# The last 64 queries of four heads as four 64x64 quarters of TensorE's array

## The chip, the cores and the metric

One of the cores of a Trainium2 chip runs the whole program. The metric is the device time in microseconds (us). The kernel before took 1368.56 us (median of 3 runs, 1368.39 to 1369.04).

## The reference

Attention in which each query keeps its 32 largest scores, and then a gated network without a nonlinearity, all in fp32. The shapes are 8 batches, 8 heads, 576 queries and keys, 64 numbers a head; 4608 tokens, 512 wide, with an inner width of 1024.

```python
scores = scale * np.matmul(q, k.transpose(0, 1, 3, 2))
kth = np.partition(scores, -top_k, axis=-1)[..., -top_k:-top_k + 1]
scores = np.where(scores >= kth, scores, -1000000000.0)
attn = softmax(scores)                  # along the keys
x = (attn @ v), heads side by side      # 4608 x 512
a = x @ w1
b = x @ w2
h = a * b @ w3
return h @ w_out
```

## The kernel before

**Slots.** Attention goes in slots of 128 rows of scores for two heads. Two heads make a pair (rows 0 to 63 of a loaded tile are the 64 numbers of one head, rows 64 to 127 those of the other; `HEADS` in line 25 are these two halves). 576 queries are four blocks of 128 and a rest of 64, so a pair has four ordinary slots (t = 0 to 3), and the rests of two pairs, four heads in all, share one slot, t == 4. It is called the shared slot here. In `SLOTS` (line 27) it stands fifth of nine, so of 144 slots 16 are shared ones, counted from 0 these are slots 4, 13, 22, ... 139.

**Scores.** `scores` (line 182) makes the 128 x 2 x 576 scores of a slot in two halves of 288 keys, each in a PSUM tile `st` of two banks; index `a` names the bank. In an ordinary slot bank 0 takes the head of rows 0 to 63 and bank 1 that of rows 64 to 127; each matmul uses 64 rows and all 128 columns of the array (line 197). In a shared slot `a` names the pair: the loaded `qt` has 128 more columns, 512 to 639, in which the host has put the rest of the first head in the upper 64 rows and left columns, and that of the second head in the lower rows and right columns, with zeros elsewhere. One matmul of all 128 rows and 128 columns (line 194) then gives both heads of a pair: the first head's queries on PSUM partitions 0 to 63, the second's on 64 to 127. A matmul in fp32 stands as two in the trace, so the four of a shared slot are eight there.

**The way of a slot.** ACT copies the scores to SBUF (`s`), one copy a half. DVE finds the 32 largest of each row (`top`, with a work tile `w`), POOL makes the threshold (`edge`), ACT and POOL mask (`pab`), ACT takes the exponentials in place, POOL and DVE invert the sums (`sums`). PE turns the weights (`tp`, `ro`), ACT copies them (`pts`, `pr`), PE multiplies them with v (`values`, tile `ro`, in tiles of 128 rows and 64 columns) and spreads the inverted sums over the partitions; ACT copies these (`rec`), and DVE multiplies both into x (`xt`).

**The order.** All engines work through their instructions in the order in which the loop of line 484 writes them. One turn of the loop takes slot i's scores, finds the top 32 of slot i-1, masks slot i-2 and turns and multiplies slot i-3. Between these, `fill` (line 447) puts in 32 matmuls a turn of the network of a batch whose attention is finished (`ab` for the first two products, `eo` for the last; lines 500, 511, 531), so that nothing of the network is left but that of the last batch, which runs alone at the end. In the first turns, before a batch is finished, weights are unpacked instead (`warm`). Three PSUM tiles, `st` for both halves and `tp`, take turns in two buffers of pool `ps_a`: the second `st` of a turn waits for ACT's copy `pts` of this turn's `tp`.

**The loads.** `load_pair` (line 172) loads q, k and v of a pair with one DMA each on SP's queue, three pairs ahead.

Of the kernel before, what the change touches and what calls it, by code (L numbers as in the profile page):

```python
# [9 lines left out]
F32 = mybir.dt.float32  # L10
# [8 lines left out]
B, H, S, D = 8, 8, 576, 64  # L19
NHP = H // 2  # L20
HS = S // 2
# [3 lines left out]
HEADS = slice(0, 64), slice(64, 128)  # L25
# [31 lines left out]
def attn_moe(ctx: ExitStack, tc: tile.TileContext, q, k, v, w1, w2, w3, w_out, out, flag, general):  # L57
# [12 lines left out]
    pe, act, dve, pool, sp = nc.tensor, nc.scalar, nc.vector, nc.gpsimd, nc.sync  # L70

    const = ctx.enter_context(tc.tile_pool(name="const", bufs=1))
    kq_p = ctx.enter_context(tc.tile_pool(name="kq", bufs=AHEAD))
# [9 lines left out]
    ident = const.tile([128, 128], F32, name="ident")  # L83
# [13 lines left out]
    if not general:  # L97
        pe, act, dve, pool, sp = (InOrder(tc, e) for e in (pe, act, dve, pool, sp))
# [70 lines left out]
    def at(x, b, *i):  # L169
        return x[(b, *i)] if isinstance(b, int) else x[(ds(b, 1), *i)].rearrange("o p n -> (o p) n")  # L170

    def load_pair(b, hp):

        qt = kq_p.tile([128, 5 * 128], F32, tag="q", name="qt")
        sp.dma_start(qt, at(q, b, hp))
        kt = kq_p.tile([128, S + 64], F32, tag="k", name="kt")
        sp.dma_start(kt, at(k, b, hp))
        vt = kq_p.tile([128, 11 * D], F32, tag="v", name="vt")
        sp.dma_start(vt, at(v, b, hp))
        return qt, kt, vt  # L180

    def scores(pairs, t):

        out = []
        for lo, hi in HALVES:
            st = ps_a.tile([128, 2, 512], F32, tag="a", name="st")
            for a in range(2):  # L190
                cut = slice(lo + 64, hi + 64) if a == 0 else slice(lo, hi)
                if t == 4:
                    qt, kt, _ = pairs[a]
                    pe.matmul(st[:, a, :HS], qt[:, 512:640], kt[:, cut], start=True, stop=True)
                else:
                    (qt, kt, _), p = pairs[0], HEADS[a]
                    pe.matmul(st[:, a, :HS], qt[p, t * 128 : (t + 1) * 128], kt[p, cut], start=True, stop=True)
            out.append(st)
        return out

    def new_s():
        return att_p.tile([128, 2, S], F32, tag="s", name="s", bufs=3)
# [49 lines left out]
    def new_weights():  # L252
        return att_p.tile([128, 2, S], F32, tag="pab", name="pab"), small.tile([128, 2], F32, tag="sums", name="sums")
# [31 lines left out]
    def take_turned(tp, ro):  # L285
        pts = att_p.tile([128, 2, 512], F32, tag="pts", name="pts", bufs=1)
        act.copy(pts, tp)
        pr = att_p.tile([128, 128], F32, tag="pr", name="pr")
        act.copy(pr, ro[:, :128])
        return pts, pr  # L290

    def values(vts, t, pts, pr, sums, ro):

        ov, rb = ro[:, 128:256], ro[:, 256:384]
        ends = t == 4
        for a, h in enumerate(HEADS):
            if ends:
                for j in range(2):
                    pe.matmul(
                        rb[h, j * 64 : j * 64 + 64], sums[:, j : j + 1].to_broadcast([128, 64]), ident[:, h], start=True, stop=True  # L300
                    )
            else:
                pe.matmul(rb[h], sums[:, a : a + 1].to_broadcast([128, 64]), ident, start=True, stop=True)
        for j in range(2 if ends else 1):
            vt = vts[j]
            for c in range(5):
                for i, h in enumerate(HEADS):
                    block = i * 4 + c if c < 4 else (((8, 10), (10, 9))[j][i] if ends else 8 + i)
                    n = slice(i * 64, i * 64 + 64) if ends else slice(0, 128)
                    rhs = pr[:, n] if c == 4 else pts[:, j if ends else i, c * 128 + n.start : c * 128 + n.stop]  # L310
                    to = ov[h, j * 64 : j * 64 + 64] if ends else ov[h]
                    pe.matmul(to, vt[:, block * D : (block + 1) * D], rhs, start=(c == 0), stop=(c == 4))
        return ov, rb
# [91 lines left out]
    if general:  # L405
# [3 lines left out]
        with tc.For_i(0, B, 1) as b:  # L409
            seen = small.tile([1, 1], I32, tag="seen", name="seen", bufs=1)  # L410
            nc.sync.dma_start(seen, flag[ds(b + 1, 1), :])
            with tc.If(nc.values_load(seen, min_val=0, max_val=1) > 0):
                kv, xs = {}, {}
                for hps, t in SLOTS:
                    for hp in hps:
                        if hp not in kv:
                            kv[hp], xs[hp] = load_pair(b, hp), new_xt()
                    s, st = new_s(), scores([kv[hp] for hp in hps], t)
                    for h in range(2):
                        take_scores(s, st, h)  # L420
                    edge = top32_exact(s)
                    pab, sums = new_weights()
                    for a in range(2):
                        mask(s, edge, pab, a)
                        exps(edge, pab, sums, a)
                    invert(sums)
                    tp, ro = turn(pab)
                    ov, rb = values([kv[hp][2] for hp in hps], t, *take_turned(tp, ro), sums, ro)
                    store_x([xs[hp] for hp in hps], t, ov, take_rb(rb))
                xt, parts = [xs[hp] for hp in range(NHP)], ([], [])  # L430
                for pair in range(2):
                    split_x(parts, xt, 0, pair)
                for _ in moe_steps(b, xt, parts, lambda f: f()):
                    pass
# [20 lines left out]
    def pairs_of(i):  # L455
        return [kv[u] for u in slots[i][0]]

    def fetch_pair(u):
        if u < B * NHP:
            kv[u] = load_pair(u // NHP, u % NHP)  # L460
# [23 lines left out]
    for p in range(-1, n_slots + 3):  # L484
        i, j, m = p + 1, p - 1, p - 2
# [28 lines left out]
        if i < n_slots:  # L514
            st = scores(pairs_of(i), slots[i][1])
            ss[i] = new_s()
            take_scores(ss[i], st, 0)
# [4 lines left out]
        if 0 <= m < n_slots:  # L522
            us, t = slots[m]
            for u in us:
                if u not in xts:
                    xts[u] = new_xt()
            ov, rb = values([kv[u][2] for u in us], t, pts, pr, pabs[m][1], ro)
            rec = take_rb(rb)
# [79 lines left out]
```

## Time and profile before

| | |
|---|---|
| median of 3 runs | 1368.56 us (1368.39 to 1369.04) |
| the profiled execution | 1368.85 us, of which the span of its instructions 1367.1 us |
| PE busy | 1269.8 us (93%) |
| DVE busy | 1156.8 us (85%) |
| ACT busy | 981.7 us (72%) |
| POOL busy | 784.6 us (57%) |
| mean granted clock of TensorE | 0.961 of full speed |

The profile is of one execution. A busy engine is one with an instruction in work. Time between instructions counts as idle, and the trace names what ended it. Idle time costs only where the engine is the one that all others come to wait for, and this differs between the start, the long middle and the end of this program.

### The profile page before, as it was taken

The numbers are of one execution on the slowest core, as the hardware profiler recorded it, in microseconds if no ns is written. First come the engines' busy times: TensorE is split into PE (matmuls) and PEld (weight loads), VectorE is DVE, ScalarE is ACT, GpSimd is POOL, SyncE is SP. The second block draws the span as 40 slices with busy tenths as digits, with TensorE's granted clock in tenths as the row PEclk, the third lists the DMA queues.
The fourth block names the chain that finished last, engine by engine and source line by source line (L and its number), as shares of the span: only waits on it lengthen the run. The fifth ranks groups of instructions, "written<-read, shape, count | busy, mean of one in ns | idle before, by whom it ended". The sixth has DMA issues, their size and how long they took to land.

```text
span 1367.1 us, 31053 instructions
## 1 busy us (share of the span) xinstructions
PE 1269.8 (93%) x11025; PEld 1101.1 (81%) x11025; DVE 1156.8 (85%) x4060; ACT 981.7 (72%) x2169; POOL 784.6 (57%) x1033
## 2 busy tenths in 40 slices
PE   2788855899999999999999999999999999999996
PEld 1444434798889998999988899989999889999996
DVE  6989898999999999898989899999899898988000
ACT  4777777777777777786777777777778777777221
POOL 3666677665665656565656565665656565646220
PEclk6889977999999999999999999999999999999998
DMA  6443430002010101001010202011111001000000
GB/s 220 109 131 100 124 104 31 31 12 68 12 59 21 49 31 40 29 21 60 17 63 12 68 12 68 12 48 32 44 36 38 31 17 64 12 19 1 18 18 21
DMA packets 34745, 65.01 MB, mean 48 GB/s; under 512 B 3860, under 2 KB 12052, under 8 KB 34580
## 3 DMA queue, kind: packets, MB, share of 16 engines
q1 hardware_dynamic: 34580, 62.93, 14.5%
q8 instruction: 89, 1.46, 0.4%
q14 instruction: 76, 0.62, 0.1%
HBM read 53.48 MB, written 9.44 MB: 46 GB/s over the span
## 4 chain that ended last, share of the span: by engine, by line
PE 79%; DVE 12%; ACT 5%; issue 2%; POOL 1%; DMA 0%; DVEq 0%; SPq 0%; POOLq 0%; ACTq 0%
PE ab L48 30%; PE eo L48 15%; PE ro L48 14%; PE st L48 11%; PE tp L48 8%; DVE w L48 5%; DVE top L48 3%; ACT pab L48 2%; DVE y L48 2%; DVE z L48 1%; ACT pts L48 1%; PE pf L48 1%; ACT y L48 1%; POOL wl L48 0%; ACT t L48 0%
## 5 line engine op out<-in xcount | busy, mean ns | idle before, releaser
L48 POOL TENSOR_TENSOR pab<-s,pab 128x576 f32<-128x576 f32 x288 | 403.2, 1422 | 251.0 <-DVE w L48 192.9
L48 DVE MAX8 top<-w 128x8 f32<-128x192 f32 (+1 forms) x1152 | 466.3, 445 | 0.0
L48 PE MATMUL ab<-xf,wh 128*128 128x288 f32 x2048 | 432.5, 299 | 0.0
L48 PEld LDWEIGHTS ab<-xf,wh 128*128 128x128 f32 x2048 | 332.8, 188 | 8.3 <-issue 7.4
L48 PE MATMUL ab<-xf,wl 128*128 128x288 f32 x1024 | 309.8, 303 | 0.0
L48 ACT ACTIVATE pab<-s,edge 128x576 f32<-128x576 f32 x288 | 208.0, 771 | 116.3 <-POOL edge L48 116.0
L48 DVE MATCH_REPLACE8 w<-top,w 128x192 f32<-128x192 f32 x864 | 288.7, 341 | 0.0
L48 PE MATMUL st<-kt,qt 64*128 64x288 f32 (+1 forms) x1152 | 206.0, 445 | 60.6 <-ACT pts L48 50.9
L48 ACT ACTIVATE pab<-pab,edge 128x576 f32<-128x576 f32 x288 | 224.8, 781 | 20.9 <-POOL pab L48 20.4
L48 PE MATMUL eo<-g,wf 128*128 128x288 f32 x1536 | 228.2, 300 | 0.0
L48 PEld LDWEIGHTS eo<-g,wf 128*128 128x128 f32 x1536 | 208.3, 188 | 7.0 <-issue 7.0
L48 PEld LDWEIGHTS st<-kt,qt 64*128 64x128 f32 (+1 forms) x1152 | 113.6, 193 | 113.7 <-ACT pts L48 59.6
L48 PEld LDWEIGHTS ab<-xf,wl 128*128 128x128 f32 x1024 | 192.2, 188 | 4.8 <-issue 4.8
L48 ACT COPY s<-st 128x576 f32<-128x576 f32 x288 | 181.8, 632 | 14.1 <-PE st L48 14.0
L48 ACT COPY pts<-tp 128x1024 f32<-128x1024 f32 x144 | 145.4, 1010 | 61.9 <-PE tp L48 57.1
L48 PE MATMUL tp<-ident,pab 128*128 128x128 f32 x1152 | 154.1, 277 | 15.6 <-ACT s L48 15.0
L48 POOL TENSOR_TENSOR g<-whole,g 128x288 fp32r<-128x288 f32 x128 | 102.8, 803 | 114.0 <-ACT g L48 110.1
L48 DVE TENSOR_TENSOR w<-w,s 128x384 f32<-128x384 f32 x288 | 159.9, 555 | 4.9
L48 PE MATMUL ro<-pts,vt 128*64 128x128 f32 (+1 forms) x2560 | 163.3, 273 | 0.0
L48 DVE TENSOR_TENSOR w<-s 128x384 f32<-128x384 f32 x288 | 155.9, 581 | 7.9 <-ACT s L48 7.9
L48 PEld LDWEIGHTS tp<-ident,pab 128*128 128x128 f32 x1152 | 135.8, 143 | 24.7 <-POOL wo L48 13.2
L48 PEld LDWEIGHTS ro<-pts,vt 128*64 128x64 f32 x2560 | 143.7, 144 | 0.0
(49 smaller groups left out, 1275.8 us busy)
## 6 DMA issues: line engine op xcount, KB each, us to landing
z<-in_w SPq DMA_DIRECT2D x64, 256.0 KB, 2.7
vt<-in_v SPq DMA_DIRECT2D x32, 352.0 KB, 3.9
qt<-in_q SPq DMA_DIRECT2D x32, 320.0 KB, 2.9
kt<-in_k SPq DMA_DIRECT2D x32, 320.0 KB, 3.5
out_t<-osb SPq DMA_DIRECT2D x64, 144.0 KB, 1.7
z<-in_wo SPq DMA_DIRECT2D x16, 256.0 KB, 5.0
flag<-missed SPq DMA_DIRECT2D x1, 0.0 KB
seen<-flag SPq DMA_DIRECT2D x1, 0.0 KB
```

Of the source, the lines that this page charges most:

```text
L48: ins = fn(*args, **kw)
```

## The change

The zero-filled copy of the rests is gone from the host's array: `qt` has 576 columns now, and the rests are its last 64. A shared slot takes eight matmuls of 64 rows and 64 columns in place of four of 128 and 128. For the first pair (a = 0) head i lies on rows i and columns i of the array's halves, as before. For the second pair head i's scores go to the other half of the columns, and so to the other half of PSUM's partitions (`HEADS[i ^ a]`). The four matmuls of a half thus lie on four different quarters of the array. In `values` the second pair's turned weights and sums are read from the swapped halves; the count and sizes of the matmuls there stay.

```diff
     def load_pair(b, hp):

-        qt = kq_p.tile([128, 5 * 128], F32, tag="q", name="qt")
+        qt = kq_p.tile([128, S], F32, tag="q", name="qt")
         sp.dma_start(qt, at(q, b, hp))
...
                 if t == 4:
                     qt, kt, _ = pairs[a]
-                    pe.matmul(st[:, a, :HS], qt[:, 512:640], kt[:, cut], start=True, stop=True)
+                    for i, p in enumerate(HEADS):
+                        pe.matmul(st[HEADS[i ^ a], a, :HS], qt[p, 512:], kt[p, cut], start=True, stop=True)
...
                     pe.matmul(
-                        rb[h, j * 64 : j * 64 + 64], sums[:, j : j + 1].to_broadcast([128, 64]), ident[:, h], start=True, stop=True
+                        rb[h, j * 64 : j * 64 + 64], sums[:, j : j + 1].to_broadcast([128, 64]), ident[:, HEADS[a ^ j]],
+                        start=True, stop=True,
                     )
...
-                    n = slice(i * 64, i * 64 + 64) if ends else slice(0, 128)
+                    n = HEADS[i ^ j] if ends else slice(0, 128)
...
     qt = _np.asarray(q).reshape(B, NHP, 2, S, D).transpose(0, 1, 2, 4, 3)
-    qp = _np.zeros((B, NHP, 2, D, 640), _np.float32)
-    qp[..., :512] = qt[..., :512]
-    qp[:, :, 0, :, 512:576] = qt[:, :, 0, :, 512:]
-    qp[:, :, 1, :, 576:] = qt[:, :, 1, :, 512:]
...
-        "in_q": c(qp.reshape(B, NHP, 128, 640)), "in_k": c(kp.reshape(B, NHP, 128, S + 64)), "in_v": c(vp.reshape(B, NHP, 128, 11 * D)),
+        "in_q": c(qt.reshape(B, NHP, 128, S)), "in_k": c(kp.reshape(B, NHP, 128, S + 64)), "in_v": c(vp.reshape(B, NHP, 128, 11 * D)),
```

This is the order on PE in the program before, in a shared slot of the second batch: the network's matmul ahead of the scores, both halves of the scores (`st` with two buffer numbers; two `qt` and `kt` are the two pairs), and the spreading of the sums behind them. Sizes are those of the result.

```order
L48 MATMUL ab_2498<-xf_2408,wh1_99 128x288
L48 MATMUL st_2513<-kt_1419,qt_1417 128x288
L48 MATMUL st_2513<-kt_2056,qt_2054 128x288 [waits DMAHW7_49,DMAHW0_49]
L48 MATMUL st_2516<-kt_1419,qt_1417 128x288 [waits Activation_49]
L48 MATMUL st_2516<-kt_2056,qt_2054 128x288
L48 MATMUL ro_2490<-ident_85,sums_2374 64x128 [waits DVE_49,Activation_49]
```

The same place now:

```order
L48 MATMUL ab_2506<-xf_2416,wh1_99 128x288
L48 MATMUL st_2521<-kt_1423,qt_1421 64x288 x2
L48 MATMUL st_2521<-kt_2064,qt_2062 64x288 [waits DMAHW7_49,DMAHW0_49]
L48 MATMUL st_2521<-kt_2064,qt_2062 64x288
L48 MATMUL st_2526<-kt_1423,qt_1421 64x288 [waits Activation_49]
L48 MATMUL st_2526<-kt_1423,qt_1421 64x288
L48 MATMUL st_2526<-kt_2064,qt_2062 64x288 x2
L48 MATMUL ro_2498<-ident_85,sums_2382 64x128 [waits DVE_49,Activation_49]
```

Each matmul has become two, the waits stand on the first of the two, and what comes before and behind is the same. On DVE, ACT and POOL no instruction moves, and on SP only the size of the q loads differs.

## Rows read from the trace of the kernel before

**Rows 1.** Stretches, with each engine's busy time, granted clock, DMA share, GB/s
```profile
core 0: us, PE busy (x) PEld busy (x) DVE busy (x) ACT busy (x) POOL busy (x), PEclk, DMA share, GB/s
0.00:259.00 259.00, 174.71 (x1010) 106.52 (x1011) 227.57 (x719) 181.55 (x429) 164.50 (x228) 0.82 0.36 109
259.00:1256.00 997.00, 997.00 (x9244) 897.67 (x9243) 915.76 (x3303) 770.90 (x1669) 594.23 (x773) 1.00 0.11 35
```
**Rows 2.** PE's waits from 0 to 259: total us, times, longest
```profile
PE st L48 <- ACT pts L48: 50.9, 17, 6.4
```
**Rows 3.** PE's waits from 259 to the end, all of them
```profile
PE ro L48 <- ACT pr L48: 0.2, 1, 0.2
```
**Rows 4.** Chain that ended last, pieces from its start: start, us, what
```profile
1.21 3.57 DMA kt<-in_k
...
43.09 1.93 DVE w L48 x3
...
167.84 0.52 DVE top L48 x2
...
246.73 1.34 DVE top L48 x2
...
251.43 1.33 PE st L48 x4
```
**Rows 5.** PE in order of time, a shared slot: start, us, what
```profile
479.53 0.29 PE L48 MATMUL ab<-xf,wh 128*128 128x288 f32 x1
479.67 2.10 PE L48 MATMUL st<-kt,qt 128*128 128x288 f32 x8
481.70 0.44 PE L48 MATMUL ro<-ident,sums 128*64 128x128 f32 x4
```
**Rows 6.** PE in order of time, the ordinary slot behind it
```profile
488.38 0.29 PE L48 MATMUL ab<-xf,wl 128*128 128x288 f32 x1
488.61 1.24 PE L48 MATMUL st<-kt,qt 64*128 64x288 f32 x8
489.78 0.44 PE L48 MATMUL ro<-ident,sums 128*64 128x128 f32 x4
490.05 1.04 PE L48 MATMUL ro<-pts,vt 128*64 128x128 f32 x16
490.92 0.39 PE L48 MATMUL ro<-pr,vt 128*64 128x128 f32 x4
```
**Rows 7.** Weight loads by shape: count, busy us, mean ns, idle before
```profile
L48 PEld LDWEIGHTS ro<-pts,vt 128*64 128x64 f32 x2560 | 143.7, 144 | 0.0
L48 PEld LDWEIGHTS st<-kt,qt 64*128 64x128 f32 x1024 | 89.8, 193 | 101.8 <-ACT pts L48 53.3 <-issue 29.9 <-ACT s L48 6.6
```
**Rows 8.** PE in order of time, slot 25, the whole and from its second round
```profile
284.19 1.29 PE L48 MATMUL st<-kt,qt 64*128 64x288 f32 x8
...
284.53 0.70 PE L48 MATMUL st<-kt,qt 64*128 64x288 f32 x4
```
**Rows 9.** DVE's waits for ACT's `rec`, 479 to 562: total, times, longest
```profile
DVE xt L48 <- ACT rec L48: 4.9, 4, 1.6
```
**Rows 10.** DVE in the shared slot that begins at 553.17
```profile
557.08 0.29 DVE L48 TENSOR_TENSOR xt<-ro,rec 128x128 f32<-128x128 f32 x1 [1.16 <-ACT rec L48]
```
**Rows 11.** ACT in the shared slot at 479.67 and the slot behind it
```profile
483.27 0.27 ACT L48 COPY rec<-ro 128x128 f32<-128x128 f32 x1 [0.51 <-PE ro L48]
...
487.19 1.02 ACT L48 COPY pts<-tp 128x1024 f32<-128x1024 f32 x1 [0.44 <-PE tp L48]
```
**Rows 12.** ACT's `pts` and PE's scores, three slots behind a shared one
```profile
503.97 1.00 ACT L48 COPY pts<-tp 128x1024 f32<-128x1024 f32 x1
...
504.75 1.24 PE L48 MATMUL st<-kt,qt 64*128 64x288 f32 x8
```
**Rows 13.** DVE's waits from 256 to 290, all of them
```profile
DVE sums L48 <- POOL sums L48: 2.0, 2, 1.1
```
**Rows 14.** ACT's `pts` in slot 25
```profile
283.67 1.00 ACT L48 COPY pts<-tp 128x1024 f32<-128x1024 f32 x1
```

## The prediction

> **What bounds the kernel now.** I read the stretches first. From 0 to 259 us PE is busy for 174.71 us of 259 and DVE for 227.57; from 259 to 1256 PE is busy for 997.00 us of 997.00, at the full granted clock of 1.00, and DVE for 915.76 [rows 1]. The table of waits says the same from the other side: until 259 PE waited 50.9 us for ACT's `pts` alone [rows 2], and from there to the end 0.2 us in all [rows 3]. The chain in order of time gives the border: its pieces are DVE's and ACT's up to 246.73, and PE's from 251.43 on [rows 4]. So what PE is spared behind the border shortens the program unless another engine becomes late; what it is spared ahead of it should not.
>
> A shared slot comes every nine slots. Two of the sixteen lie at the start (slots 4 and 13, at 42 and 168 us), one right behind the border (slot 22, at 259), and thirteen in the stretch that PE fills.
>
> **The scores of a shared slot.** Before, eight instructions of 288 columns follow each other: from the start of the first to the start of what comes next 481.70 - 479.67 = 2.03 us, 0.25 us each [rows 5]. In an ordinary slot eight instructions of 288 columns take 489.78 - 488.61 = 1.17 us [rows 6], too little for eight after each other: two are at work at once, one on each half of the rows, in four rounds. Halves of the columns do so too: the sixteen of `ro<-pts`, with 128 moving columns, take 490.92 - 490.05 = 0.87 us, and alone they would need 16 x 0.25 x 128/288 = 1.78 us [rows 6]. The order on the engine puts two instructions of one tile ahead of the two of the other tile, and they still overlap, so an instruction that must wait for its own tile does not hold up one of another tile.
>
> The change makes sixteen instructions, four on each quarter. Nothing in this trace runs on quarters; what it shows is rows overlapping and columns overlapping, each with different moving data and at full rate. If both hold at once, the four quarters run four rounds, as an ordinary slot does. I take that as the likeliest. The price, with the entry into the tiles included, is measured from the last matmul of the network: 481.70 - 479.53 = 2.17 us for a shared slot [rows 5] and 489.78 - 488.38 = 1.40 us for an ordinary one [rows 6], so 0.77 us less. The first round of an ordinary slot is longer than the later ones, 284.53 - 284.19 = 0.34 us [rows 8], since the second weights are not there yet; weights of 64 columns load in 144 ns and of 128 in 193 [rows 7], so the new slot is 0.05 us better here. Two more tiles to start cost a few hundredths at most, an estimate from the 0.05 us. Gain per shared slot: between 0.77 and 0.82 us; I take 0.80. The bound on the other side, quarters that do not overlap, is a rival below.
>
> One statement goes further than these rows: the Trainium skill ("TensorE: Matmul & The Clock Gate", Part 3) says that row and column tiles compose, with some 4 ns for each further tile; by it the two further tiles cost under 0.01 us and the gain is 0.81 us. No run here shows it yet.
>
> **Does the gain stay?** In the thirteen slots the question is what restarts from PE and what does not. DVE stands idle in a shared slot until ACT's `rec` arrives, 1.16 us in the one at 553.17 [rows 10] and up to 1.6 us in four such waits [rows 9]. ACT's `rec` itself waited 0.51 us for PE's `ro`, and in the next slot ACT's `pts` 0.44 us for PE's `tp` [rows 11]. With PE 0.80 us earlier, `rec` is 0.80 earlier, and DVE's idle time there falls to 1.16 - 0.80 = 0.36 us: it still waits for PE, and so its long chain of the next slots starts earlier by the same amount. That matters, since three slots behind a shared one `pts` ends at 503.97 + 1.00 = 504.97 and the second half of the scores wants its buffer at 504.75 + 0.34 + 0.24 = 505.33 (a first and a later round): only 0.36 us of slack [rows 8, 12]. Both move together, and the slack stays. Over the long run DVE has room: 915.76 of 997 us [rows 1], so 81 us idle, and the change takes away some 11.
>
> Slot 22 is different. From 256 to 290 DVE waits twice, 2.0 us in all, and only for POOL [rows 13]; it is catching up from the start and does not begin earlier when PE does. In slot 25 `pts` ends at 283.67 + 1.00 = 284.67 [rows 14], and the second half of the scores follows at 284.53 + 0.24 = 284.77 [rows 8]. PE can come earlier by 0.1 us there and no more: of slot 22's 0.80 us I count 0.1.
>
> Slots 4 and 13: the chain has DVE at 43.09 and at 167.84 [rows 4], and PE waits for `pts` behind both. I count 0; the bounds are 0 and 0.8 each, if a wait turns out to hang on these scores.
>
> **The loads.** Each q is 288 KB, not 320. All but the first are three pairs ahead, under PE's work. The first scores wait for k, 3.57 us [rows 4], while q and k, 640 KB, come together; a twentieth of that is 0.18 us at most, and 0.1 is my value (0 to 0.18). In `values` counts and sizes stay, only the halves that are read differ: 0.
>
> **The sum.** 13 x 0.80 + 0.1 + 0.1 = 10.6 us. The profiled execution took 1368.85 us, 1.75 more than its span, and becomes 1358.25. The median is 0.29 lower than that execution: 1358.0 us.
>
> **Rivals.**
>
> Two at a time. In each half the first two matmuls, heads of one pair, use different rows and write the same bank of PSUM, on different partitions; in ordinary slots the two row halves always write different banks. If the banks, not the partitions, decide, only two of the quarters that differ in their bank run together: sixteen instructions in eight rounds, the 2.03 us of before. On top come the entry into the tiles, (488.61 - 488.38) - (479.67 - 479.53) = 0.09 us [rows 5, 6], and half of the 0.10 us by which a first round is longer: 13 x 0.14 = 1.8 us, less the 0.1 of the load, so 1370.3 us. The Trainium skill has this as a rule ("TensorEngine Tiling (Array Packing)", Restrictions and Gotchas, Gotcha 1): different row tiles cannot access the same PSUM bank at the same time. By it the sum would be this rival's. Against it speaks that on any one partition the two writers here have different banks, just as in an ordinary slot. No row of this trace has two row halves in one bank, so it keeps a chance of 0.11.
>
> One at a time, the case that ends slower. If an instruction on a quarter has to wait until the one on the neighbouring quarter is through, be it for the same rows or the same columns, sixteen go after each other: 16 x 0.25 = 4.0 us in place of 2.03, with the 0.14 some 2.1 us more per shared slot, and 14 x 2.1 = 29 us: 1397 us. It decides from the first shared slot on, and the scores would then take twice as long as before. Against it: halves that share all columns, and halves that share all rows, both overlap now [rows 6]. Chance 0.05.
>
> The quarters overlap, and the gain is taken back by DVE's chain. If something in the chain from `rec` over DVE, POOL and ACT to `pts` does not move with PE, the buffer of the second half is late from the third slot on, and a shared slot keeps only the slack of 0.36 us: 13 x 0.36 + 0.2 = 4.9 us, 1363.7 us. For it: in some slots DVE has no idle time at all, and 0.36 us is all that stays of its wait at 553. Against it: that wait, as far as the rows go, ends with PE. Chance 0.07.
>
> **How the numbers follow.** My forecast, four at a time and the gain kept, has 0.77. Its own range is 1355.5 (0.82 us kept fourteen times, and up to 1.5 us at the start) to 1360.0 (0.70 us if the start of four tiles costs a tenth more). The range is 1355.5 to 1366.0: it holds this case and the one in which DVE takes the gain back, 0.84 together, less a little that falls outside. Differences of 0.2%, 2.7 us, are about what can be told from no change. Faster by more than that: 0.77 + 0.07 = 0.84. Within: two at a time, 0.11. Slower: one at a time, 0.05.
>
> **What would show it.** Right, if the sixteen `st` instructions of a shared slot in the middle take about 1.1 to 1.2 us from the first to the start of `ro`, if the slot is then some 8.15 us long and not 488.61 - 479.67 = 8.94 [rows 5, 6], and if PE from 259 on still waits for next to nothing. In slot 25 PE should wait some 0.7 us for `pts`, for the first time. DVE's wait for `rec` in the shared slot that now begins at 553 should be 0.3 to 0.4 us. Wrong, if the sixteen take 2 us or 4, which is the first rival or the second; or if PE waits for `pts` in the third slot behind each shared one, which is the third. If the start up to slot 22 is shorter by more than 0.3 us, I was wrong about what its chain hangs on.

## The result and the profile after

The changed kernel takes 1356.16 us (median of 6 runs, 1355.88 to 1356.86), the kernel before 1368.80 in the same comparison (median of 6 runs). The ratio is 0.9909, with a 95% interval of 0.9898 to 0.9919: 12.6 us less, where 10.6 were forecast.

A shared slot of the changed kernel, on PE in order of time (start, us, what), the counterpart of [rows 5]:

```profile
477.35 0.29 PE L48 MATMUL ab<-xf,wh 128*128 128x288 f32 x1
477.58 1.20 PE L48 MATMUL st<-kt,qt 64*64 64x288 f32 x16
478.71 0.44 PE L48 MATMUL ro<-ident,sums 128*64 128x128 f32 x4
...
550.27 1.20 PE L48 MATMUL st<-kt,qt 64*64 64x288 f32 x16
```

Sixteen instructions take 478.71 - 477.58 = 1.13 us to the next work, where eight took 2.03. From the network's last matmul it is 478.71 - 477.35 = 1.36 us against 2.17: 0.81 us less, 0.01 more than forecast. The distance from this shared slot to the next is 550.27 - 477.58 = 72.69 us, where it was 553.17 - 479.67 = 73.50 before ([rows 5], and the row of 553.17 below): the same 0.81 us over nine slots, so nothing of it is given back in between. All thirteen shared slots behind slot 22 gain it, each within 0.01 us.

That four run at once can be seen in the starts. A window of this slot that ends 0.04 us behind the first score (at 477.62) holds four instructions, and the next four begin 0.29 us behind the first:

```profile
477.58 0.47 PE L48 MATMUL st<-kt,qt 64*64 64x288 f32 x4
...
477.87 0.42 PE L48 MATMUL st<-kt,qt 64*64 64x288 f32 x4
```

Some of the following rows are of windows that end inside a slot's scores; only their first numbers, the starts, are used. The kernel before, with the starts of slots 22, 31 and 58 and the end of slot 25's scores:

```profile
259.11 0.41 PE L48 MATMUL st<-kt,qt 128*128 128x288 f32 x1
...
285.41 0.40 PE L48 MATMUL ro<-ident,sums 128*64 128x64 f32 x6
...
332.66 0.65 PE L48 MATMUL st<-kt,qt 128*128 128x288 f32 x2
...
553.17 2.10 PE L48 MATMUL st<-kt,qt 128*128 128x288 f32 x8
```

Slots 22 and 31 in the changed kernel:

```profile
258.75 0.47 PE L48 MATMUL st<-kt,qt 64*64 64x288 f32 x4
...
332.20 0.70 PE L48 MATMUL st<-kt,qt 64*64 64x288 f32 x6
```

From slot 22 to slot 31 it is 73.55 us before and 73.45 after: of the 0.81 us that slot 22 itself gained, 0.10 stays. Where the rest goes is on PE in slots 23 and 25 of the changed kernel:

```profile
266.80 1.54 PE L48 MATMUL st<-kt,qt 64*128 64x288 f32 x8
268.27 0.44 PE L48 MATMUL ro<-ident,sums 128*64 128x128 f32 x4
...
283.24 0.76 PE L48 MATMUL st<-kt,qt 64*128 64x288 f32 x4
284.17 0.76 PE L48 MATMUL st<-kt,qt 64*128 64x288 f32 x4 [0.17 <-ACT pts L48]
284.86 0.46 PE L48 MATMUL ro<-ident,sums 128*64 128x64 f32 x8
```

Slot 23's scores take 268.27 - 266.80 = 1.47 us in place of an ordinary 1.17 [rows 6], and slot 25's 284.86 - 283.24 = 1.62 in place of 285.41 - 284.19 = 1.22 [rows 8]: 0.7 us lost because the second halves wait for ACT's `pts`. PE's waits from 258.5 to the end have one line more than [rows 3], the first of these two. It names only the 0.17 us in slot 25 in which no instruction was in work any more. The second line is that of the weight loads (PEld), from 258 to 300, and shows both waits:

```profile
PE st L48 <- ACT pts L48: 0.2, 1, 0.2
PEld st L48 <- ACT pts L48: 1.1, 2, 0.6
```

In the kernel before, the weight loads of the same stretch waited for `pts` once:

```profile
PEld st L48 <- ACT pts L48: 0.2, 1, 0.2
```

From 256 to 290 DVE waits as before, twice, 2.0 us in all, and only for POOL (the row is word for word that of [rows 13]). In the later shared slots, at 480.58 and at 553.28, its wait for `rec` is shorter, 0.83 in place of 1.6 and 0.35 in place of 1.16 [rows 9, 10], but it is still there. ACT's wait for `tp` behind a shared slot is 0.43 us, where it was 0.44 [rows 11]:

```profile
480.58 0.29 DVE L48 TENSOR_TENSOR xt<-ro,rec 128x128 f32<-128x128 f32 x1 [0.83 <-ACT rec L48]
...
553.28 0.29 DVE L48 TENSOR_TENSOR xt<-ro,rec 128x128 f32<-128x128 f32 x1 [0.35 <-ACT rec L48]
...
556.89 1.02 ACT L48 COPY pts<-tp 128x1024 f32<-128x1024 f32 x1 [0.43 <-PE tp L48]
```

PE fills the middle as before (stretch, busy time of PE, PEld, DVE, ACT, POOL, granted clock, DMA share, GB/s), and DVE has 71 us left in it:

```profile
258.75:1245.00 986.25, 986.05 (x9357) 885.08 (x9358) 915.49 (x3302) 770.51 (x1668) 594.32 (x773) 1.00 0.11 34
```

One thing was not forecast at all: the end. In the chain of waits the piece of PE's last transpose (`wp`, start and us) stands at

```profile
1354.19 0.12 PE wp L48
```

in the kernel before, whose span is 1367.1, and at

```profile
1343.08 0.12 PE wp L48
```

in the changed one, whose span is 1354.3. What follows is the same in both: the flag that says whether a second, general version of the whole kernel must run is written and read back, the program branches over that version, and it closes. From the start of this piece to the end of the span it is 12.9 us before and 11.2 after. So the spans differ by 12.8 us, of which 1354.19 - 1343.08 = 11.1 lie ahead of the last transpose and 1.7 behind it.

### The profile page after: what moved, and what is told of

It reads as the page before. It is cut to its first block, busy times and chain, and to the rows that moved or that the text cites. A ratio compares the mean times of both kernels' runs of the same rounds, so it can differ in the third digit from the quotient of the medians.

```text
span 1354.3 us, 31309 instructions
## 1 busy us (share of the span) xinstructions
PE 1253.2 (93%) x11153; PEld 1081.8 (80%) x11153; DVE 1156.7 (85%) x4060; ACT 981.6 (72%) x2169; POOL 785.0 (58%) x1033
## 3 DMA queue, kind: packets, MB, share of 16 engines
q8 instruction: 90, 1.47, 0.5%
## 4 chain that ended last, share of the span: by engine, by line
PE 77%; DVE 13%; ACT 5%; issue 2%; POOL 2%; DMA 0%; DVEq 0%; SPq 0%; POOLq 0%; ACTq 0%
PE ab L48 29%; PE eo L48 15%; PE ro L48 14%; PE st L48 10%; PE tp L48 8%; DVE w L48 5%; DVE top L48 4%; ACT pab L48 2%; DVE y L48 2%; DVE z L48 2%; ACT pts L48 1%; ACT y L48 1%; POOL wl L48 1%; ACT t L48 1%; POOL y L48 0%
## 5 line engine op out<-in xcount | busy, mean ns | idle before, releaser
L48 PE MATMUL st<-kt,qt 64*128 64x288 f32 (+1 forms) x1280 | 191.2, 444 | 61.0 <-ACT pts L48 51.7
L48 PEld LDWEIGHTS st<-kt,qt 64*128 64x128 f32 (+1 forms) x1280 | 97.8, 181 | 115.5 <-ACT pts L48 61.6
```

Source lines behind the costliest of these rows:

```text
L48: ins = fn(*args, **kw)
```

## The experiments

**Two quarters in place of four.** The second pair's heads stay in their own half of the columns.

```diff
-                        pe.matmul(st[HEADS[i ^ a], a, :HS], qt[p, 512:], kt[p, cut], start=True, stop=True)
+                        pe.matmul(st[p, a, :HS], qt[p, 512:], kt[p, cut], start=True, stop=True)
...
```

(In `values`, not shown, the second pair's weights and sums are read from the unswapped halves again.)

> The changed kernel, but the second pair's heads keep their own half of the columns (st[p, a] and the unswapped reads in values): sixteen instructions of 64x64 in a shared slot, on two quarters instead of four. Theory (each quarter works through its own instructions, the fullest quarter sets the time): eight rounds of 0.24 us, from the first score to the spreading of the sums 2.1 us in place of 1.13, 0.97 us more in each of 13 shared slots; about 1369 us, the time of the kernel before or a little over. Rival (the gain comes from smaller weights and fewer zeros, not from four quarters at once): 1.13 us again, 1356 us. Rival (two row halves in one bank of PSUM shut each other out): sixteen rounds, 4 us, about 1395 us.

1369.0 us (median of 11 runs), ratio to the kernel before 0.9999 (0.999 to 1.0008): the whole gain is gone. PE in a shared slot, and a window of it that ends 0.1 us behind the first score:

```profile
553.55 0.29 PE L48 MATMUL ab<-xf,wh 128*128 128x288 f32 x1
553.77 2.16 PE L48 MATMUL st<-kt,qt 64*64 64x288 f32 x16
555.86 0.33 PE L48 MATMUL ro<-ident,sums 128*64 128x128 f32 x2
...
553.77 0.46 PE L48 MATMUL st<-kt,qt 64*64 64x288 f32 x2
```

The same sixteen instructions take 555.86 - 553.77 = 2.09 us, eight rounds. With the entry it is 555.86 - 553.55 = 2.31 us, 0.14 more than before's 2.17, the price that the prediction worked out for two at a time. That the time is just that of the kernel before is a balance: 13 x 0.14 = 1.8 us more in the shared slots, and 1.5 us less behind the last transpose (11.4 in place of 12.9, see the end of the program below). Neither the smaller weights nor the zeros that are left out are what gains; four quarters at once are. And the two matmuls of a pair, on different rows, write the same bank on different partitions here as in the changed kernel, and the last row shows the first two beginning together. The rule of the Trainium skill ("TensorEngine Tiling (Array Packing)", Restrictions and Gotchas) that different row tiles cannot use one bank at the same time does not hold in this form; by it these two could not have begun together. Two row halves in one bank on the same partitions were not tried.

**Scores of the shared slots twice.** The four matmuls of a half are issued a second time into the same place.

```diff
-            for a in range(2):
+            for a in (0, 1, 0, 1) if t == 4 else (0, 1):
```

> The changed kernel, with the scores of each shared slot computed twice in a row (the four matmuls of a half, then the same four again into the same place): 32 instructions on four quarters. Theory that four quarters at once is the whole price: four more rounds of 0.24 us, 2.1 us from the first score to the spreading of the sums in place of 1.13, 13 x 0.97 = 12.6 us more, about 1369 us. Rival, that part of the 1.13 us is no streaming (loading of weights, starting): less than 0.97 us more per slot if the second pass hides behind the first, more if the loads of 32 weights do not keep up (they are 129 ns each).

1369.18 us (median of 10 runs), ratio 1.0004 (0.9995 to 1.0014).

```profile
553.62 2.17 PE L48 MATMUL st<-kt,qt 64*64 64x288 f32 x32
555.72 0.44 PE L48 MATMUL ro<-ident,sums 128*64 128x128 f32 x4
```

2.10 us in place of 1.13: sixteen more instructions cost 0.97 us, four rounds. So the quarters stream at full rate, 0.24 us a round as in an ordinary slot, and the loads of the weights, sixteen more of them, are hidden. Sixteen instructions that are added on four quarters cost 0.97 us, about half of the 2.09 that sixteen take on two.

**Another order of the eight matmuls.** A quarter's two halves of the keys follow each other, then comes the next quarter.

```diff
...
+            for a in range(2):
+                qt, kt, _ = pairs[a]
+                for i, p in enumerate(HEADS):
+                    for st, (lo, hi) in zip(out, HALVES):
+                        cut = slice(lo + 64, hi + 64) if a == 0 else slice(lo, hi)
+                        pe.matmul(st[HEADS[i ^ a], a, :HS], qt[p, 512:], kt[p, cut], start=True, stop=True)
...
```

> The changed kernel with the eight matmuls of a shared slot in another order: a quarter's two halves of the keys follow each other, and only then comes the next quarter, so that the fourth quarter's first instruction stands behind twelve others. Theory that instructions waiting for their own quarter hold nobody up, however many they are: 1.13 us as before, 1356 us. Rival, that PE takes only one or two waiting instructions out of the way: the quarters start one after another, up to 0.24 to 0.5 us later each, 1.4 to 2.6 us for the scores, 1360 to 1375 us.

1356.87 us (median of 4 runs), ratio 0.991 (0.9895 to 0.9925).

```profile
550.65 1.22 PE L48 MATMUL st<-kt,qt 64*64 64x288 f32 x16
551.80 0.44 PE L48 MATMUL ro<-ident,sums 128*64 128x128 f32 x4
...
550.65 0.49 PE L48 MATMUL st<-kt,qt 64*64 64x288 f32 x4
```

1.15 us, 0.02 more than in the changed kernel. The last row is of a window that ends at 550.72: within 0.07 us four instructions have begun. An instruction that stands behind twelve others of other quarters starts with them nearly at once. How far ahead PE looks beyond that was not tried.

**The wide q.** All of q's 640 columns are loaded again, the last 64 of them zeros.

```diff
-        qt = kq_p.tile([128, S], F32, tag="q", name="qt")
+        qt = kq_p.tile([128, S + 64], F32, tag="q", name="qt")
...
```

> The changed kernel, but q is loaded with 640 columns again (the last 64 are zeros and not read). Theory that the first scores started 0.38 us earlier because the first q is smaller and that this stays: the first scores start at 4.9 us instead of 4.53, 0.3 to 0.4 us more at the end, 1356.5 us. Rival, that the lead of the start is another load's or chance: 4.5 us and 1356.2 us.

1356.46 us (median of 4 runs), ratio 0.9904 (0.9888 to 0.9919); the first scores start at

```profile
4.71 1.81 PE L48 MATMUL st<-kt,qt 64*128 64x288 f32 x6 [4.71 <-DMA kt<-in_k]
```

Between the two theories, and the other profiles say why: with the narrow q the first scores started at 4.53, 4.59, 4.64, 4.67 and 4.73 us, with the wide one at 4.62, 4.71 and 4.91 (without the two runs that put transposes ahead of them). A tenth of a us for the load, as the prediction had it, is possible and not resolved. It does not matter: in the same runs slot 22 began at 258.5 to 259.1 us with the wide q and at 258.5 to 259.2 with the narrow one. No gain or loss at the start can be told from this spread.

**Quarters in the ordinary slots too.** If a first round is shorter with weights of 64 columns, the other 128 slots can have it.

```diff
-                    pe.matmul(st[:, a, :HS], qt[p, t * 128 : (t + 1) * 128], kt[p, cut], start=True, stop=True)
+                    for i, r in enumerate(HEADS):
+                        pe.matmul(st[r, a, :HS], qt[p, t * 128 + i * 64 : t * 128 + i * 64 + 64], kt[p, cut], start=True, stop=True)
```

> The changed kernel, and the ordinary slots take quarters too: each matmul of 64 rows and 128 columns becomes two of 64 and 64 on the two halves of the columns, sixteen instructions on four quarters. Theory that the streaming stays four rounds and that only the first round is shorter, since weights of 64 columns are loaded sooner: 0.04 to 0.05 us less in each of some 108 ordinary slots behind the start, 4.3 to 5.4 us, about 1351.5 us. Rival, that both column halves reading the same keys, or twice the instructions, cost as much as that: 1356 us or more.

1351.95 us (median of 4 runs), ratio 0.9875 (0.986 to 0.989), 4.2 us less than the changed kernel's median; its four times, 1351.24 to 1353.27, all lie below the changed kernel's lowest, 1355.88. An ordinary slot, and the start of its second round:

```profile
484.29 0.29 PE L48 MATMUL ab<-xf,wl 128*128 128x288 f32 x1
484.51 1.20 PE L48 MATMUL st<-kt,qt 64*64 64x288 f32 x16
485.64 0.44 PE L48 MATMUL ro<-ident,sums 128*64 128x128 f32 x4
...
484.81 0.42 PE L48 MATMUL st<-kt,qt 64*64 64x288 f32 x4
```

The second round of the ordinary slot of [rows 6] in the kernel before:

```profile
488.95 0.41 PE L48 MATMUL st<-kt,qt 64*128 64x288 f32 x2
```

From the network's matmul to the next work it is 1.35 us, in place of 1.40 [rows 6]. The difference is in the first round, 484.81 - 484.51 = 0.30 us in place of 488.95 - 488.61 = 0.34: 0.04 us a slot, and 108 x 0.04 = 4.3 us. Weight loads by shape in this kernel: 135 ns each, where those of 128 columns took 193 [rows 7]:

```profile
L48 PEld LDWEIGHTS st<-kt,qt 64*64 64x64 f32 x2304 | 73.5, 135 | 127.5 <-ACT pts L48 64.0 <-issue 28.5 <-ACT s L48 7.3
```

**The end of the program**, in three runs: the changed kernel and the kernel before, each with 16 transposes that nobody reads ahead of the first scores (in the general version that is branched over, too), and the kernel before as it is. The place in a block of 64 is a guess of mine at what could matter.

```diff
+    pad = ps_m.tile([128, 512], F32, tag="mm", name="pad")
+    for _ in range(16):
+        pe.transpose(pad[:, :128], ident, ident)
```

> The changed kernel with 16 transposes of the unit matrix that nobody reads, on PE while it waits for the first load; PE's program gets 31 instructions longer, so that its last ones lie at the place in a block of 64 at which those of the kernel before lie (20 before, 52 in the changed kernel, 19 here). Theory that the 1.6 us by which the end of the program (behind the last matmul of the network) is shorter in the changed kernel hang on where PE's last instructions lie: the end takes 12.8 us again instead of 11.2, about 1357.8 us. Rival, that it is chance or has another cause: 11.2 us, 1356.2 us.

> The kernel before with the same 16 transposes ahead of the first scores: its last PE instructions then lie at 51 of 64, as those of the changed kernel do (52). Theory of the place: the end behind the last matmul takes 11.2 us instead of 12.9, about 1367.4 us. Rival, chance or another cause: 12.9 us, 1369 us.

> The kernel before, unchanged, for a second profile of it. Theory that the end's length belongs to the program: 12.9 us behind the last matmul again; the first scores start at 4.5 to 4.9 us. Rival, that both vary from run to run: an end of about 11.2 us, as the five other profiles have.

The last transpose in the chain of the kernel before, run again (span 1366.3), and of the kernel before with its code shifted (span 1365.0):

```profile
1353.54 0.12 PE wp L48
```

```profile
1354.10 0.12 PE wp L48
```

And of the changed kernel with its code shifted (span 1354.6):

```profile
1343.81 0.12 PE wp L48
```

So from the start of this piece to the end of the span it is 12.8 us for the kernel before (12.9 the first time), 10.9 for the same with shifted code, and 10.8 for the changed kernel with shifted code. The times: the shifted kernel before took 1366.93 us (median of 10 runs), ratio 0.9989 (0.9979 to 0.9998), 1.7 us less although it does more; the shifted changed kernel 1356.31 (4 runs), as before the shift; the kernel before, once more, 1368.07 (one run). The long end belongs to the kernel before as it stands, and not to chance, since it came again in a second profile, and was gone when 31 unused instructions of PE shifted its code, in one profile and, by the median of ten runs, in the time. That it is the place of the code, and not something else that these instructions bring with them, is the likeliest reading; another shift of the kernel before was not tried. My rule for it, the place within blocks of 64 instructions, is wrong: the changed kernel should have got the long end by it and did not.

What the traces do show is where the time goes. Their records of semaphores, which no view above lists, have PE answer the first release of the closing barrier 2.1 us behind SP, ACT and DVE in both long profiles, and within 0.1 us of them in the other eight. In the long ones 16 KB on an instruction queue start to move within 0.1 us of this release; but they do so in the shifted kernel before as well, where PE answers at once, so this transfer alone is not the cause. Which place is a bad one, and what PE does there, stays open.

## Why the prediction was right

**Four quarters at once.** Right, to 0.01 us in the slot: the trace had rows overlapping and columns overlapping, and together they overlap as well. The run with two quarters and the run with twice the scores show the price from both sides, 0.96 and 0.97 us for four rounds more. Both the rival of two at a time and that of one at a time are excluded; the first has its price in the run with two quarters. The Trainium skill's statement that row and column tiles compose ("TensorE: Matmul & The Clock Gate", Part 3) is borne out here: the four quarters begin within 0.04 us and run together. The estimate of 0.81 us worked out by it is what was measured, but 0.80 was forecast without it, and 0.01 us does not tell the two apart.

One sign was worked out wrongly. The slot was to be 8.15 us long from its first score to the next slot's, and it is 8.03 (485.61 - 477.58 in the row below, of the slot behind the shared one): the entry into the tiles, 0.09 us, now comes ahead of the shared slot's first score, where before it came ahead of the next slot's. The forecast of the gain had this entry in it, the sign had not.

```profile
485.61 1.24 PE L48 MATMUL st<-kt,qt 64*128 64x288 f32 x8
```

**The gain stays in the thirteen slots.** Right: 13 x 0.81 = 10.5 us where 10.4 were forecast. DVE's idle time at the shared slot fell from 1.16 to 0.35 us, forecast 0.36, and PE waits for nothing there. The rival that DVE's chain takes the gain back is excluded for a gain of this size; how a gain that used up the 0.35 us that remain would fare was not tried.

**Slot 22.** Right in size: 0.10 us of 0.81 stayed, and PE waits for `pts` as forecast. The place was half right: 0.3 us of the 0.7 are lost in slot 23, which the prediction did not look at, and 0.4 in slot 25.

**The start.** The two shared slots there were counted as 0. With their scores computed twice, slot 22 still began at 258.96 us, no later than the 258.5 to 259.2 of the other profiles, so their price does not reach it. The changed profile comes to slot 22 earlier by 0.36 us at the first score and by 0.46 at the network's matmul ahead of it (258.52 in place of 258.98). By the prediction's own sign, 0.3 us, that would speak against what it says of the start. But two profiles of the unchanged kernel before differ by 0.6 us there (259.11 and 258.51), so the sign was finer than what one profile can tell.

**What was missed.** The sum had no term for the end of the program. It let the stretch behind the last matmul stand as it was, since the change touches nothing in it, and this is 1.7 us of the 2.0 by which the forecast was off. In the two profiles the 12.8 us are 10.5 in the thirteen slots, 0.1 in slot 22, 0.5 of lead at the start and 1.7 at the end; the forecast had 10.4, 0.1 and 0.1 for the first three. So the mechanism was right, and that the time came out near the lower end of the range is the end's doing and, by some tenths, the start's. A slip in the working: the upper end of the forecast's own range, 1360.0, should be 1359.5 by its own term (13 x 0.70 = 9.1 us).

## What to carry to other kernels

Small matmuls that leave three quarters of the array empty can run four at a time, if they are placed so that each quarter gets an equal share; giving two heads the other half of PSUM's partitions was the whole difference here, 2.09 against 1.13 us for the same instructions. The price of such a change is read from a stretch that already uses halves, by its rounds; its worth is decided by whether the other engines' waits restart from PE, which is seen from what ended their idle time just behind the place. Where halves already fill the array, quarters still spared 0.04 us a slot, all of it in the first round; that it is the smaller weights, 135 ns to load in place of 193, which are there sooner is the likely reason and was not tested apart.

## What the runs showed of the hardware that was not expected

The same closing instructions took 12.8 and 12.9 us from the last transpose on in two profiles of one program and 10.8 to 11.4 in one profile each of eight others, and 31 unused instructions of PE at the program's start took 1.9 us off it (12.8 to 10.9). In this comparison 1.7 of the 12.8 us came from there, and not from the change of the scores. A difference of one or two us between two programs can thus lie in a stretch that no edit touched, and is looked for there before it is put down to the edit.
